# Attention, routed experts and a Fourier block on one core: softmax and weight decoding kept in PSUM, logits left in their scale, small work on ScalarE

## The chip, the cores and the metric

The kernel runs on one core of one Trainium2 chip. The metric is the device time of one execution in microseconds; what is compared is the median over runs. TensorE (PE) multiplies, VectorE (DVE), ScalarE (ACT) and GpSimd (POOL) work on tiles of up to 128 partitions, and SyncE (SP) issues most of the DMAs. Matrix results land in PSUM, in eight banks of 512 f32 columns; everything else lies in SBUF.

## The reference

Three blocks follow one another, on 8 batches of 576 rows with 8 heads of 64 columns (512 in all):

```python
# 1: attention against keys and values that are means over 8 rows (72 of them)
k_p, v_p = mean of 8 rows of k, v
scores = q @ k_p.T / 8;  attn = softmax(scores) (the sum has 1e-9 added);  x = attn @ v_p
# 2: one expert per row
logits = x @ w_gate                        # 8 experts
fresh = argmax(logits);  e = fresh where row 0 or sigmoid(x @ w_local) < 0.5, else that of the row before
p = softmax(logits);     out = p[e] * (relu(x @ w1[e]) @ w2[e])
# 3: Fourier mixing and a feed-forward block
u = out + real(fft over rows and columns of out);  un = layernorm(u)
result = u + relu(un @ w_ch1) @ w_ch2
```

The weights of block 3 arrive as 64-bit floats.

## The kernel before, in words

The program has two parts. **The first** does blocks 1 and 2 for batches 0 to 6, with the expert that the first row of a batch chooses; the attention of a batch runs beside the experts of the batch before. A loop over a number of further pairs of batch and expert, which is known only at run time, stands behind it. **The second** does the experts of batch 7, then block 3 batch by batch.

In the first part `moe` is a generator of 34 steps per batch, and `attention` one of some 21; the main loop advances the one beside the other, so the program's text interleaves them. The order on each engine is then set by a scheduler from the text and the data that each instruction needs. Each engine works through its order and waits in it.

Attention goes by five row tiles of 128 (one of 64). `att_A` turns q by TensorE and copies it (L225). `att_B` multiplies with the pooled keys into the tile `sc`, two PSUM banks with one buffer (L234 to L236), and forms the softmax on VectorE: maximum (L239), difference into the SBUF tile E (L242), Exp on ScalarE in place (L244), sum (L246), the addition of 1e-9 and a scale (L247), reciprocal (L248) and product (L249). For batches from 1 on, the result is split into a high half in f16 (ScalarE, L255) and a low half (VectorE, L256), and a DMA turns both (L258). `att_D` multiplies with V, `att_L` forms eight logits and the local gate's (L303, L304) and scales them by the column iv (L305). `route` chooses the experts from them, compares the gate with a constant (L336) and forms the softmax over experts (L341). L372 to L376 give each row its coefficient.

Experts: `moe1_f` multiplies with w1 in high and low halves into a bank of the tag `mm` (two buffers); ScalarE writes the high half of the result (L460), VectorE the low one (L461), which frees the bank. `moe2_t` multiplies with w2, `store_y` scales by the coefficient (L514), copies columns 0 and 256 into `ycol` (L515), and stores. The coefficients are scaled three times per batch first (L556). Meanwhile expert weights of the next batch are loaded, their maximum taken (VectorE, L401), scaled and rounded (ScalarE, L427, L428), and their low halves formed on POOL (L429). `pool_kv` forms the pooled keys and values on POOL (L169 to L171).

Decoding: five times per batch, `decode_parts` turns a piece of 64-bit weights into f32 by integer operations: Abs on ScalarE (L629), a maximum that also keeps the largest (L631), shift and mask (L632), and two merges with the upper and lower words (L634, L635), all in the SBUF tile dt; the next piece is loaded behind that (L616).

In PSUM the first part holds `mm` twice, `a1` twice, `sc` (two banks), `hg`, and `et`, which only batch 0 uses.

Of the kernel before, what the change touches and what calls it, by code (L numbers as in the profile page):

```python
# [9 lines left out]
F32 = mybir.dt.float32  # L10
# [13 lines left out]
E_TOP = 14  # L24
# [39 lines left out]
def attention_moe_fourier_kernel(ctx: ExitStack, tc: tile.TileContext, aps, out, B=8):  # L64
# [43 lines left out]
    def small(shape, dt, tag):  # L108
        return sm.tile(shape, dt, tag=tag, name=tag)
# [8 lines left out]
    wg_inv = const.tile([128, 1], F32, name="wg_inv")  # L118
    eps = const.tile([128, 1], F32, name="eps")
# [30 lines left out]
    kraw, kp, kbd, vs, vmax = {}, {}, {}, {}, {}  # L150
# [38 lines left out]
    def prep_v(b):  # L189
# [11 lines left out]
        TS(out=inv, in0=inv, scalar1=0.125, scalar2=None, op0=ALU.mult)  # L201

# [28 lines left out]
    def att_B(b, i):  # L231
# [8 lines left out]
        e = mt([128, 8, 72], F32, "E")  # L240
        e4 = e[:n].rearrange("p (a h) k -> p a h k", a=2)
        TT(out=e4, in0=s4, in1=mx[:n].to_broadcast([n, 2, 4, 72]), op=ALU.subtract)  # L242

        S.activation(out=e[:n], in_=e[:n], func=ACTF.Exp, scale=2.0 ** -6)  # L244
        es = small([128, 8, 1], F32, "es")
        V.tensor_reduce(out=es[:n, :, 0], in_=e[:n], axis=AX.X, op=ALU.add)  # L246
        TS(out=es[:n], in0=es[:n], scalar1=1e-9, scalar2=2.0 ** -E_TOP if b else 1.0, op0=ALU.add, op1=ALU.mult)  # L247
        V.reciprocal(out=es[:n], in_=es[:n])  # L248
        V.tensor_tensor(out=e[:n], in0=e[:n], in1=es[:n].to_broadcast([n, 8, 72]), op=ALU.mult)  # L249
        if b == 0:  # L250
            E[b, i] = e
            return
        hl = ehl_t[n_e[0] % 2]
        n_e[0] += 1
        S.copy(out=hl[:n, 0, :, 0:72], in_=e[:n])  # L255
        V.tensor_tensor(out=hl[:n, 1, :, 0:72], in0=e[:n], in1=hl[:n, 0, :, 0:72], op=ALU.subtract)  # L256
# [38 lines left out]
    def att_L(b, i):  # L295
# [9 lines left out]
        TS(out=lg[b][:n, i, :], in0=lg[b][:n, i, :], scalar1=iv[b][:n], scalar2=None, op0=ALU.mult)  # L305
# [19 lines left out]
    def route(b):  # L325
# [10 lines left out]
        TS(out=m, in0=lg[b][:, :, 8], scalar1=GATE_THR, scalar2=None, op0=ALU.is_le)  # L336
# [4 lines left out]
        S.activation(out=ex, in_=ex, func=ACTF.Exp)  # L341
# [4 lines left out]
        er = sm.tile([1, 576], F16, tag="r_er", name="r_er", bufs=1)  # L346
        n0 = 0
        for r, n in ((row, 320), (row2, 256)):
            mb = sm.tile([1, 320], F32, tag="r_mb", name="r_mb", bufs=1)
# [155 lines left out]
    def store_y(b, add):  # L505
        def done(i, n, po, c):
# [8 lines left out]
            V.tensor_copy(out=ycol[:n, i, :, b], in_=t[:n, 0:512:256])  # L515
# [4 lines left out]
    def moe(b, decs=()):  # L520
# [34 lines left out]
        for s in (p_all[:, b, 5:6], wsc[b, 0][0], wsc[b, 1][0]):  # L555
            TS(out=c, in0=c, scalar1=s, scalar2=None, op0=ALU.mult)  # L556
# [710 lines left out]
```

## Time and profile before

| | us |
|---|---|
| median of 3 runs (1571.8 to 1578.5) | 1575.95 |
| the profiled execution | 1575.51 |
| its span, first to last instruction | 1573.6 |
| VectorE busy | 1141.8 (73%) |
| TensorE busy, matmul | 1369.7 (87%) |
| ScalarE busy | 562.0 (36%) |
| POOL busy | 407.5 (26%) |

The span is that of the profiled execution; 1.9 us lie around it. An engine's busy time is a sum over stages with different limits, so a stage is read by itself, with its own windows and waits. In the timelines and groups, a line such as "E<-sc,mx" names the tile written and those read. An instruction's duration holds the time in which it stood still after its start.

### The profile page before, as it was taken

The numbers are of one execution on the slowest core, as the hardware profiler recorded it, in microseconds if no ns is written. First come the engines' busy times: TensorE is split into PE (matmuls) and PEld (weight loads), VectorE is DVE, ScalarE is ACT, GpSimd is POOL, SyncE is SP. The second block draws the span as 40 slices with busy tenths as digits, with TensorE's granted clock in tenths as the row PEclk, the third lists the DMA queues.
The fourth block names the chain that finished last, engine by engine and source line by source line (L and its number), as shares of the span: only waits on it lengthen the run. The fifth ranks groups of instructions, "written<-read, shape, count | busy, mean of one in ns | idle before, by whom it ended". The sixth has DMA issues, their size and how long they took to land.

```text
span 1573.6 us, 25049 instructions
## 1 busy us (share of the span) xinstructions
PE 1369.7 (87%) x9674; PEld 846.5 (54%) x9674; DVE 1141.8 (73%) x2292; ACT 562.0 (36%) x1007; POOL 407.5 (26%) x465
## 2 busy tenths in 40 slices
PE   3777888778878889679499999999999999999997
PEld 3444444344434545245356666666666666666664
DVE  5896999988989988648487667575668666577442
ACT  1354555444636465525242222222222122223120
POOL 3562726363675322245301001010101001000000
PEclk9688989888988999888799999999999999999999
DMA  8648568677886757343835335160704325153010
GB/s 162 191 121 231 147 207 212 186 190 208 197 228 165 204 155 233 97 139 108 134 99 108 54 70 92 51 110 21 123 20 104 59 67 95 50 133 76 11 44 27
DMA packets 245954, 193.97 MB, mean 123 GB/s; under 512 B 185255, under 2 KB 191271, under 8 KB 244807
## 3 DMA queue, kind: packets, MB, share of 16 engines
q1 hardware_dynamic: 230198, 172.21, 45.0%
q0 software_dynamic: 10272, 10.41, 2.7%
q10 hardware_dynamic: 5360, 9.70, 1.7%
q8 instruction: 78, 1.28, 0.3%
q14 instruction: 46, 0.37, 0.1%
HBM read 111.83 MB, written 47.37 MB: 101 GB/s over the span
## 4 chain that ended last, share of the span: by engine, by line
PE 47%; DMA 6%; DVE 2%; issue 1%; ACT 0%; SPq 0%; DVEq 0%; ACTq 0%
PE mm L914 19%; PE s L981 10%; PE et L981 5%; PE hg L981 5%; DMA xhl<-un 3%; PE a L864 2%; PE mm L456 2%; DMA out_dram<-c 2%; PE a L863 1%; PE a L871 1%; DMA dd<-fw_dram 1%; PE a L752 1%; DVE c L919 0%; PE hg L457 0%; DMA c<-u_dram 0%
## 5 line engine op out<-in xcount | busy, mean ns | idle before, releaser
L919 DVE TENSOR_TENSOR c<-mm,c 128x512 f32<-128x512 f32 x180 | 122.6, 686 | 151.1 <-PE mm L914 146.1
L456 PE MATMUL mm<-xhl,w0h 128*128 128x512 f16 x512 | 178.7, 417 | 57.9 <-DVE hl L461 33.3
L914 PEld LDWEIGHTS <-wr 128*128 128x128 f16 x1728 | 168.9, 98 | 61.9 <-issue 24.0
L766 POOL DMA_DIRECT2D yb<-y_dram x42 | 26.8, 651 | 477.3 <-DVE pt L816 391.9
L914 PEld LDWEIGHTS <-ex 128*128 128x128 f16 x1296 | 125.6, 98 | 24.6 <-issue 5.7
L981 PEld LDWEIGHTS <-hl 128*128 128x128 f16 x864 | 83.8, 98 | 94.9 <-issue 1.6
L981 PEld LDWEIGHTS <-hh 128*128 128x128 f16 x864 | 84.5, 98 | 88.5 <-issue 2.4
L914 PE MATMUL mm<-xhl,wr 128*128 128x256 f16 x864 | 107.5, 275 | 23.8 <-DMA xhl<-un 23.8
L924 ACT COPY c<-mm 128x512 f32<-128x512 f32 x72 | 41.4, 584 | 183.7 <-PE mm L914 158.9
L914 PE MATMUL mm<-xhl,ex 128*128 128x256 f16 x864 | 106.6, 274 | 0.0
L456 PE MATMUL mm<-xhl,w0l 128*128 128x512 f16 x256 | 106.1, 414 | 0.1
L456 PEld LDWEIGHTS <-w0h 128*128 128x128 f16 x512 | 53.0, 104 | 96.2 <-issue 47.9
L930 ACT ACTIVATE hl<-c 128x512 f16<-128x512 f32 x72 | 45.3, 629 | 163.8 <-DVE c L919 163.8
L486 PE MATMUL mm<-w1h,hh 128*128 128x512 f16 x256 | 99.0, 387 | 1.0 <-DVE hl L461 0.9
L486 PE MATMUL mm<-w1h,hl 128*128 128x512 f16 x256 | 98.6, 385 | 0.0
L486 PE MATMUL mm<-w1l,hh 128*128 128x512 f16 x256 | 98.6, 385 | 0.0
L429 POOL TENSOR_TENSOR w0l<-wr,w0h 128x512 f16<-128x512 f32 x56 | 67.2, 1223 | 115.3 <-ACT w0h L428 29.6
L457 PE MATMUL hg<-xhl,w0h 128*128 128x64 f16 x512 | 91.9, 205 | 0.0
L930 ACT ACTIVATE hh<-c 128x512 f16<-128x512 f32 x72 | 44.6, 629 | 119.3 <-DVE c L919 119.2
L427 ACT ACTIVATE wr<-wr,wscale 128x512 f32<-128x512 f32 x120 | 79.9, 712 | 14.7 <-DVE wscale L134 11.9
L429 POOL TENSOR_TENSOR w1l<-wr,w1h 128x512 f16<-128x512 f32 x64 | 73.0, 1168 | 33.9 <-ACT w1h L428 26.5
L401 DVE TENSOR_REDUCE wmax<-wr 128x1 f32<-128x1024 f32 x64 | 76.8, 1208 | 2.0 <-DMA wr<-in_moe_w_dram 2.0
(294 smaller groups left out, 3229.9 us busy)
## 6 DMA issues: line engine op xcount, KB each, us to landing
wr<-in_moe_w_dram SPq DMA_DIRECT2D x32, 1024.0 KB
dd<-in_moe_w_ch_dram SPq DMA_DIRECT2D x32, 512.0 KB
kraw<-in_k_dram SPq DMA_DIRECT2D x8, 1152.0 KB
vraw<-in_v_dram SPq DMA_DIRECT2D x8, 1152.0 KB
xs_dram<-xhl SPq DMA_DIRECT2D x8, 1152.0 KB
y_dram<-y ACTq DMA_DIRECT2D x32, 256.0 KB
fw_dram<-dt SPq DMA_DIRECT2D x32, 256.0 KB
u_dram<-yb SPq DMA_DIRECT2D x32, 256.0 KB
```

Of the source, the lines that this page charges most:

```text
L401: V.tensor_reduce(out=m[:, c:c + 1], in_=tc_, axis=AX.X, op=ALU.max, apply_absolute_value=True)
L427: S.activation(out=t[:, sl], in_=t[:, sl], func=ACTF.Copy, scale=s)
L429: G.tensor_tensor(out=l[:, sl], in0=t[:, sl], in1=h[:, sl], op=ALU.subtract)
L456: P.matmul(po, lhsT=ww[:, c], rhs=x[:, j, kk, 64:576], start=st, stop=sp)
L457: P.matmul(go, lhsT=ww[:, c], rhs=x[:, j, kk, 0:64], start=st, stop=sp)
L486: P.matmul(po, lhsT=hx[:, f, c0:c0 + n], rhs=ww[:, 512 * f:512 * f + 512], start=(f == 0 and t == 0), stop=(f == 7 and t == 2))
L864: P.matmul(o, lhsT=fd[2][gw, n, :M], rhs=tabs[nm][gw, 1, i], start=False, stop=True)
L914: P.matmul(o[:, q], lhsT=fw1[n][:, w, kk, f], rhs=unT[b][x][:, u, kk, :], start=(kk == 0 and i == 0), stop=(kk == 1 and i == 2))
L919: TT(out=c, in0=x, in1=y, op=ALU.add)
L924: S.copy(out=c, in_=o)
L930: S.activation(out=d[0], in_=c, func=ACTF.Relu)
L981: P.matmul(acc[i], lhsT=h[:, x, hf, q, 128 * i:128 * i + 128], rhs=fw2[w][hf][:, 512 * f:512 * f + 512], start=(f == 0 and hf == 0 and n = ...
```

## The change

Five edits, all in the first part's functions:

- `att_B` keeps difference, Exp, sums and product in the PSUM tile `sc`; only batch 0 writes its result into SBUF. The split reads PSUM, and `sc` comes free with the low half.
- `decode_parts` works in a PSUM bank of the tag `et` (one buffer); only the last merge writes SBUF.
- The logits keep their scale: the instruction of L305 goes. The gate's threshold is scaled for each batch instead (one product of two columns, and one for all), and the routing's Exp takes iv as its scale.
- The columns for `ycol` and the three scalings of the coefficients go from VectorE to ScalarE.
- Three small tiles of the routing move from the lasting pool to that of the first part.

```diff
-        e = mt([128, 8, 72], F32, "E")
-        e4 = e[:n].rearrange("p (a h) k -> p a h k", a=2)
-        TT(out=e4, in0=s4, in1=mx[:n].to_broadcast([n, 2, 4, 72]), op=ALU.subtract)
-        S.activation(out=e[:n], in_=e[:n], func=ACTF.Exp, scale=2.0 ** -6)
-        es = small([128, 8, 1], F32, "es")
-        V.tensor_reduce(out=es[:n, :, 0], in_=e[:n], axis=AX.X, op=ALU.add)
-        TS(out=es[:n], in0=es[:n], scalar1=1e-9, scalar2=2.0 ** -E_TOP if b else 1.0, op0=ALU.add, op1=ALU.mult)
-        V.reciprocal(out=es[:n], in_=es[:n])
-        V.tensor_tensor(out=e[:n], in0=e[:n], in1=es[:n].to_broadcast([n, 8, 72]), op=ALU.mult)
+        TT(out=s4, in0=s4, in1=mx[:n].to_broadcast([n, 2, 4, 72]), op=ALU.subtract)
+        S.activation(out=sc[:n, :, 0:288], in_=sc[:n, :, 0:288], func=ACTF.Exp, scale=2.0 ** -6)
+        sums = sc[:n, 0, 288:296]
+        V.tensor_reduce(out=sums.rearrange("p (a h) -> p a h", a=2), in_=s4, axis=AX.X, op=ALU.add)
+        TS(out=sums, in0=sums, scalar1=1e-9, scalar2=2.0 ** -E_TOP if b else 1.0, op0=ALU.add, op1=ALU.mult)
+        es = small([128, 2, 4, 1], F32, "es")
+        V.reciprocal(out=es[:n].rearrange("p a h o -> p (a h o)"), in_=sums)
         if b == 0:
-            E[b, i] = e
+            E[b, i] = e = mt([128, 8, 72], F32, "E")
+            TT(out=e[:n].rearrange("p (a h) k -> p a h k", a=2), in0=s4, in1=es[:n].to_broadcast([n, 2, 4, 72]), op=ALU.mult)
             return
+        TT(out=s4, in0=s4, in1=es[:n].to_broadcast([n, 2, 4, 72]), op=ALU.mult)
...
-        S.copy(out=hl[:n, 0, :, 0:72], in_=e[:n])
-        V.tensor_tensor(out=hl[:n, 1, :, 0:72], in0=e[:n], in1=hl[:n, 0, :, 0:72], op=ALU.subtract)
+        hi, lo = (hl[:n, x, :, 0:72].rearrange("p (a h) k -> p a h k", a=2) for x in range(2))
+        S.copy(out=hi, in_=s4)
+        TT(out=lo, in0=s4, in1=hi, op=ALU.subtract)
...
+        TT(out=thr[b], in0=s, in1=wg_thr, op=ALU.mult)
...
-        TS(out=lg[b][:n, i, :], in0=lg[b][:n, i, :], scalar1=iv[b][:n], scalar2=None, op0=ALU.mult)
...
-        TS(out=m, in0=lg[b][:, :, 8], scalar1=GATE_THR, scalar2=None, op0=ALU.is_le)
+        TS(out=m, in0=lg[b][:, :, 8], scalar1=thr[b], scalar2=None, op0=ALU.is_le)
...
-        S.activation(out=ex, in_=ex, func=ACTF.Exp)
+        S.activation(out=ex, in_=ex, func=ACTF.Exp, scale=iv[b])
...
-            V.tensor_copy(out=ycol[:n, i, :, b], in_=t[:n, 0:512:256])
+            S.copy(out=ycol[:n, i, :, b], in_=t[:n, 0:512:256])
...
-            TS(out=c, in0=c, scalar1=s, scalar2=None, op0=ALU.mult)
+            S.activation(out=c, in_=c, func=ACTF.Copy, scale=s)
...
-        S.activation(out=t.bitcast(F32), in_=hi.bitcast(F32), func=ACTF.Abs)
+        pf = bank([128, 512], "et")
+        pi = pf.bitcast(I32)
+        S.activation(out=pf, in_=hi.bitcast(F32), func=ACTF.Abs)
...
-        TS(out=t.bitcast(F32), in0=t.bitcast(F32), scalar1=TINY_HI, scalar2=0.0, op0=ALU.max, op1=ALU.max, accum_out=fmax[:, c:c + 1])
-        TS(out=t, in0=t, scalar1=3, scalar2=0x3FFFFFF8, op0=ALU.logical_shift_left, op1=ALU.bitwise_and)
+        TS(out=pf, in0=pf, scalar1=TINY_HI, scalar2=0.0, op0=ALU.max, op1=ALU.max, accum_out=fmax[:, c:c + 1])
+        TS(out=pi, in0=pi, scalar1=3, scalar2=0x3FFFFFF8, op0=ALU.logical_shift_left, op1=ALU.bitwise_and)
...
-        STT(out=t, in0=hi, scalar=-0x40000000, in1=t, op0=ALU.bitwise_and, op1=ALU.bitwise_or)
-        STT(out=t, in0=lo, scalar=29, in1=t, op0=ALU.logical_shift_right, op1=ALU.bitwise_or)
+        STT(out=pi, in0=hi, scalar=-0x40000000, in1=pi, op0=ALU.bitwise_and, op1=ALU.bitwise_or)
+        STT(out=t, in0=lo, scalar=29, in1=pi, op0=ALU.logical_shift_right, op1=ALU.bitwise_or)
```

The scheduler gives each engine of the first part another order. VectorE before, in batch 4, between the products of the second and third row tile's softmax (the L249 is the second tile's, L239 and L242 the third's; E and ehl hold the softmax and its halves):

```order
L249 TENSOR_TENSOR E<-E,es 128x576
L365 COPY code_all<-a_3507 64x1
L515 COPY ycol<-y 128x2
L635 SCALAR_TENSOR_TENSOR dt<-dd,dt 128x512
L371 TENSOR_TENSOR r_oh<-tab_81,code_all 128x40
L239 TENSOR_REDUCE mx<-sc 128x8
L256 TENSOR_TENSOR ehl_97<-E,ehl_97 128x8x72
L372 TENSOR_TENSOR r_oh<-r_oh,r_ex 128x40
L242 TENSOR_TENSOR E<-sc,mx 128x576
```

VectorE with the change, at the same place (L248 to L261 the second tile's, L242 the third's; lines are those of the changed kernel, where L248 is the sum, L256 the product, L261 the low half, and L637 to L640 decode):

```order
L248 TENSOR_REDUCE sc<-sc 128x8
L249 TENSOR_SCALAR sc<-sc 128x8
L251 RECIPROCAL es<-sc 128x8
L256 TENSOR_TENSOR sc<-sc,es 128x2x288
L637 TENSOR_SCALAR et,fmax<-et 128x512
L261 TENSOR_TENSOR ehl_98<-sc,ehl_98 128x8x72
L638 TENSOR_SCALAR et<-et 128x512
L640 SCALAR_TENSOR_TENSOR et<-dd,et 128x512
L242 TENSOR_REDUCE mx<-sc 128x8
L641 SCALAR_TENSOR_TENSOR dt<-dd,et 128x512
L244 TENSOR_TENSOR sc<-sc,mx 128x2x288
```

Before, the third tile's maximum stands ahead of the second's low half; now it stands behind it, since the scores of a tile enter `sc` only when the low half before has been read. The copy of `ycol` is gone from between. On TensorE some 30 large multiplications of the experts (tag `mm`) now stand between the scores of two tiles of one batch, on average over the 28 such pairs of batches 1 to 7, where it was 24.

ScalarE before, in batch 4, from the second tile's Exp (L244) to the scaling of expert weights (L427):

```order
L629 ACTIVATE dt<-dd 128x512
L244 ACTIVATE E<-E 128x576
L514 ACTIVATE y<-mm,cm 128x512
L225 COPY qT<-a_3495 128x512
L517 DMA y_dram<-y 128x512
L427 ACTIVATE wr_3016<-wr_3016,wscale_3489 128x512
L255 CAST ehl_97<-E 128x8x72
```

ScalarE with the change, about the same place (L635 is decoding's Abs, L246 the Exp, L260 the high half, L519 the `ycol` copy, L560 the scaling of the coefficients):

```order
L518 ACTIVATE y<-mm,cm 128x512
L519 COPY ycol<-y 128x2
L521 DMA y_dram<-y 128x512
L246 ACTIVATE sc<-sc 128x2x288
L560 ACTIVATE cm<-cm,p_all 128x5
L560 ACTIVATE cm<-cm,winv_3179 128x5
L635 ACTIVATE et<-dd 128x512
L260 CAST ehl_98<-sc 128x8x72
```

The copies now follow the scaling L518 ahead of its store, and the scalings of the coefficients stand ahead of an Abs and a high half in ScalarE's queue.

## Rows read from the trace of the kernel before

**Rows 1.** Stretches: busy us (instructions) of PE, PEld, DVE, ACT, POOL; granted clock; DMA share; GB/s.
```profile
90.00:655.00 565.00, 463.60 (x3712) 253.69 (x3708) 501.53 (x1043) 298.25 (x528) 261.39 (x266) 0.90 0.70 190
...
800.00:1573.00 773.00, 755.45 (x4974) 497.61 (x4971) 491.05 (x950) 184.78 (x324) 39.07 (x68) 1.00 0.33 70
```

**Rows 2.** Waits of TensorE, 90 to 655 us: us in total, times, longest.
```profile
PE mm L456 <- DVE hl L461: 33.3, 9, 10.2
PE a L285 <- DVE vs L413: 12.0, 5, 3.1
PE a L285 <- ACT vs L412: 11.3, 3, 6.6
PE a L303 <- DVE xhl L290: 10.2, 8, 3.0
PE sc L236 <- DVE E L242: 6.1, 4, 2.8
```

**Rows 3.** Groups of VectorE, 90 to 655 us: busy us, mean ns, idle time before.
```profile
L634 DVE SCALAR_TENSOR_TENSOR dt<-dd,dt 128x512 int32<-128x512 int32 x32 | 31.7, 991 | 0.1
L256 DVE TENSOR_TENSOR ehl<-E,ehl 128x576 f16<-128x576 f32 x28 | 27.7, 990 | 2.7 <-ACT ehl L255 2.4
L635 DVE SCALAR_TENSOR_TENSOR dt<-dd,dt 128x512 int32<-128x512 int32 x32 | 24.8, 774 | 0.1
L249 DVE TENSOR_TENSOR E<-E,es 128x576 f32<-128x576 f32 x28 | 23.7, 847 | 0.1
L631 DVE TENSOR_SCALAR_CACHE_REDUCE dt<-dt 128x512 f32<-128x512 f32 x32 | 21.8, 680 | 21.4 <-ACT dt L629 21.2
L556 DVE TENSOR_SCALAR cm<-cm,winv 128x5 f32<-128x5 f32 x16 | 21.3, 1330 | 0.3
L242 DVE TENSOR_TENSOR E<-sc,mx 128x576 f32<-128x576 f32 x28 | 21.0, 749 | 0.3
...
L305 DVE TENSOR_SCALAR lg<-lg,iv 128x9 f32<-128x9 f32 x28 | 19.1, 682 | 0.1
...
L632 DVE TENSOR_SCALAR dt<-dt 128x512 int32<-128x512 int32 x32 | 16.8, 524 | 0.2
L247 DVE TENSOR_SCALAR es<-es 128x8 f32<-128x8 f32 x28 | 11.6, 414 | 0.1
L515 DVE COPY ycol<-y 128x2 f32<-128x2 f32 x28 | 9.2, 327 | 4.1 <-ACT y L514 4.1
L556 DVE TENSOR_SCALAR cm<-cm,p_all 128x5 f32<-128x5 f32 x8 | 7.3, 915 | 0.0
L305 DVE TENSOR_SCALAR lg<-lg,iv 64x9 f32<-64x9 f32 x7 | 7.0, 996 | 0.0
...
L299 DVE TENSOR_TENSOR iv<-p_all,wg_inv 128x1 f32<-128x1 f32 x7 | 4.0, 565 | 0.0
```

**Rows 4.** Timeline of VectorE, 192 to 204 us: start, length.
```profile
192.56 9.40 DVE L556 TENSOR_SCALAR cm<-cm,winv 128x5 f32<-128x5 f32 x2
```

**Rows 5.** Timeline of POOL, the same stretch.
```profile
196.34 6.70 POOL L429 TENSOR_TENSOR w1l<-wr,w1h 128x512 f16<-128x512 f32 x6
```

**Rows 6.** One line, whole span: minimum, median and maximum ns.
```profile
L247 DVE TENSOR_SCALAR es<-es x40: 133/164/1239, 31.9 to 609.5; 128x8 f32<-128x8 f32 x32, 64x8 f32<-64x8 f32 x8
```

**Rows 7.** Group of ScalarE, 90 to 655 us: busy us, mean ns, idle time before.
```profile
L341 ACT ACTIVATE r_ex<-r_ex 128x40 f32<-128x40 f32 x7 | 1.7, 237 | 2.4 <-DVE r_ex L340 2.3
```

**Rows 8.** Timeline of VectorE, low half of two tiles.
```profile
89.21 0.74 DVE L256 TENSOR_TENSOR ehl<-E,ehl 64x576 f16<-64x576 f32 x1
...
591.04 0.75 DVE L256 TENSOR_TENSOR ehl<-E,ehl 128x576 f16<-128x576 f32 x1
```

**Rows 9.** Timeline of TensorE, scores of three tiles.
```profile
83.06 1.23 PE L236 MATMUL sc<-kbd,qT 128*128 128x144 f32 x8
...
577.32 1.22 PE L236 MATMUL sc<-kbd,qT 128*128 128x144 f32 x8 [1.54 <-DVE code_all L365]
...
590.23 1.25 PE L236 MATMUL sc<-kbd,qT 128*128 128x144 f32 x8
```

More of the change, by code (lines that the diff above doesn't have):

```diff
@@ L118, in attention_moe_fourier_kernel @@
     wg_inv = const.tile([128, 1], F32, name="wg_inv")
+    wg_thr = const.tile([128, 1], F32, name="wg_thr")
     eps = const.tile([128, 1], F32, name="eps")
@@ L147, in absmax @@
         return across(m, tag)
-    kraw, kp, kbd, vs, vmax = {}, {}, {}, {}, {}
+    kraw, kp, kbd, vs, vmax, thr = {}, {}, {}, {}, {}, {}
     def load_kv(b):
@@ L201, in prep_v @@
         TS(out=inv, in0=inv, scalar1=0.125, scalar2=None, op0=ALU.mult)
+        thr[b] = small([128, 1], F32, "thr")
+        TT(out=thr[b], in0=s, in1=wg_thr, op=ALU.mult)
     qt, qT, E, ET, xhl, lg, iv = {}, {}, {}, {}, {}, {}, {}
@@ L345, in route @@
             P.matmul(r[:, s0:s0 + n], lhsT=f16[:n, j:j + 1], rhs=ident16[:n, :n], start=True, stop=True)
-        er = sm.tile([1, 576], F16, tag="r_er", name="r_er", bufs=1)
+        er = pool["sb"].tile([1, 576], F16, tag="r_er", name="r_er", bufs=1)
         n0 = 0
         for r, n in ((row, 320), (row2, 256)):
-            mb = sm.tile([1, 320], F32, tag="r_mb", name="r_mb", bufs=1)
+            mb = pool["sb"].tile([1, 320], F32, tag="r_mb", name="r_mb", bufs=1)
             TS(out=mb[:, 0:n], in0=r[:, 0:n], scalar1=0.0, scalar2=None, op0=ALU.is_equal)
@@ L1035, in count_extras @@
     def count_extras():
-        oh = sm.tile([128, B, 5, 8], F32, tag="x_oh", name="x_oh", bufs=1)
+        oh = pool["sb"].tile([128, B, 5, 8], F32, tag="x_oh", name="x_oh", bufs=1)
         cnt = small([128, B, 8], F32, "x_cnt")
@@ L1071, in attention_moe_fourier_kernel @@
     pow2_scale(absmax(wg_raw, 128), wg_inv, s, 0)
+    TS(out=wg_thr, in0=s, scalar1=8.0 * GATE_THR, scalar2=None, op0=ALU.mult)
     split(wg_hl[:, :, 0], wg_hl[:, :, 1], wg_raw, s)
```

## The prediction, as it was put on record

> **What bounds the kernel now.** I read the stretches first. The first part, from 90 us to 655 us, has VectorE busy for 501.5 of 565 us and TensorE for 463.6 at a granted clock of 0.90; from 800 us on TensorE is busy for 755.5 of 773 us at full clock [rows 1]. The change touches the first part alone, so the end part stays as it is, and the question is what 565 us become.
>
> Second, who waits for whom. Of TensorE's 101.4 us of idle time in that stretch (565 less 463.6), 33.3 us ended with VectorE's low half of the hidden rows (L461), 12.0 with the low half of V (L413), 10.2 with the low half of x (L290) and 6.1 with the subtraction that frees the score banks (L242): 61.6 us. A further 11.3 us ended with the scaling of V on ScalarE, which takes its scale from VectorE [rows 2]. So VectorE is the engine that the others wait for, but it is not the only bound: TensorE has 82% of the stretch itself.
>
> Third, what VectorE spends its time on. The two kinds of small scaling, on 9 and 5 columns, take 682 to 1330 ns each, as long as a subtraction of 576 columns does (749) [rows 3]. The timeline shows why: from 192.56 us two scalings of five columns took 9.40 us together, to 201.96, while POOL ran six subtractions of weights back to back from 196.34 to 203.04 (1.12 us each), behind additions; the second scaling got through as the fifth of the six ended [rows 4, 5]. L249 and L256 with both inputs in SBUF average 847 and 990 ns, though L242, with one input in PSUM, takes 749 for the same width [rows 3]. So VectorE stands still beside POOL in instructions that read two SBUF tensors and in the small ones that scale one, and those that read PSUM are spared: no group of rows 3 with a PSUM input has such a mean. [...]
>
> **The sum on VectorE, in this stretch** [rows 3, 6]:
> - L305, scaling of the logits, is gone: 19.1 + 7.0 = 26.1 us.
> - L556, 24 scalings of the coefficients, goes to ScalarE: 21.3 + 7.3 = 28.6 us.
> - L515, kept columns, goes to ScalarE: 9.2 us for the full tiles. Together 63.9 us.
> - L247 on PSUM: 28 x 414 ns become 28 x 164, its median, for its work is the same and only POOL's share goes: 7.0 us.
> - L249 and L256: to 749 ns, L242's price: 23.7 + 27.7 become 2 x 21.0, so 9.4 us. L242 and the reductions have one SBUF input already: nothing.
> - L634 and L635: 31.7 + 24.8 become 2 x 32 x 680 ns = 43.5, so 13.0 us (680 is L631's price at this width).
> - L632 gets dearer. In SBUF it has 524 ns on average; nothing in this trace runs it in PSUM, and the nearest row, on the same tile and of the same width, is L631 with 680: 32 x 156 ns = 5.0 us more. The bounds are 0 more and 32 x 467 = 14.9 more (L634's 991).
> - Added: the gate's threshold, one product of two SBUF columns per batch, like L299: 7 x 565 ns = 4.0 us. The one for all batches is a single small instruction ahead of the stretch.
>
> That is 63.9 + 7.0 + 9.4 + 13.0 - 5.0 - 4.0 = 84.3 us of 501.5. For results that VectorE writes into PSUM the trace has no row; I take L242's price (PSUM in) and L631's (width), as the nearest. If PSUM were no better than today's means, the 29.4 us of the softmax and decoding terms would go and 54.9 would be left; below that nothing is known that would take more, save L632's bound.
>
> [...] L242 reads PSUM and takes 749 ns; L256, with both inputs in SBUF and the same width, took 740 and 750 ns where POOL left it alone [rows 3, 8], so a move into PSUM costs nothing that these rows show. [...]
>
> ScalarE takes the 24 scalings and 34 copies at about 237 ns, the price of its small Exp (L341): 13.7 us beside 298 us of work in 565 [rows 1, 7]. That hides in its idle 267 us; without that cover it would cost the 13.7. Its Exp, Abs and high half now read or write PSUM: I take no change, and bound it at a tenth of a us on 100 instructions, 10 us either way, under the same cover. The first scaling waits for the routing on VectorE, with casts, Abs and copies queued behind it on ScalarE; today the routing's Exp waits so, for 2.4 us in seven batches [rows 7]; even ten times that would fit into the idle time, and nothing is taken for it. The copies stand ahead of the stores of y, which no engine reads in this part. Decoding's single "et" bank costs nothing: the next piece of weights is loaded only behind L635, which ends the bank's use too. No DMA is added; SP's order moves transposes by a place or two.
>
> **What is late next.** The score banks were freed by L242; now they are held until the low half is written (L256's place). Today the next scores on TensorE start before that: by 6.9 us at the first pair of tiles of one batch, by 1.6 at the last of the 26 (of 28 pairs) where it is so [rows 8, 9]; over the 28 pairs it is 155 us, 5.5 each. That wait is new on TensorE, and matrix multiplications of the experts queue behind it. Three things take it back. The chain from the end of the scores to the low half's end, 13.3 us at the tile of 577.32 us [rows 8, 9] and 14 on average over 35, loses its own 0.6 us (16.4 us over 28 tiles); as VectorE's queue has 17% less work in it, the rest falls by about 2.2 us; and the new order of instructions puts on average 30 instead of 24 large multiplications between two such scores, 1.5 us or so. What is left is 1.0 to 1.2 us per pair, and I take 1.0: 28 us.
>
> So on the path: TensorE's 61.6 + 11.3 = 72.9 us of waits go, as VectorE gets 12 us of room in each of seven batches, and 28 us come: 45 us. 565 would become 520, with TensorE at 89% and VectorE at 80%, which is possible. The profiled execution took 1575.5 us (span 1573.6 and 1.9 around it), 0.4 under the median of the three runs: 1575.5 - 45 = 1530.5, say **1531 us**.
>
> **Rivals.**
> - *All of it passes.* If VectorE alone paces the stretch and TensorE's new wait hides in idle time, 84 us go: 1491; a rising granted clock (0.90 here) may add a few. For it: 89% busy. Against it: TensorE would have to be busy 96% of what is left.
> - *The waits move.* POOL's work stays, and other instructions with two SBUF inputs (the routing's, L331 to L376) meet the same rows of subtractions. The scalings' blocked part is about 45 us (54.7 less 59 instructions at 0.164, L247's median); if half comes back, the saving is 62 us, and TensorE's waits fall by 73 x 62/84 = 54; less the 28 of the new wait: 26 us, 1550. For it: what holds VectorE is POOL's work, which stays. Against it: few such instructions are left.
> - *The score banks become the bound: slower.* If the chain of the softmax stays as long as it is, for it waits on three queues, and only the order's 1.5 to 2 us help, each pair costs 3.5 us: 98 us of new waits against 73 gone, 25 us slower: 1600. It decides at 73/28 = 2.6 us per pair. For it: the score banks have one buffer. Against it: the order leaves six more multiplications between, and VectorE has less to do.
> - *No change.* If transfers pace it (their share is 0.70 over the stretch [rows 1]), idle time moves to them: 1570 to 1580. Against it: TensorE hardly waits for one.
>
> **Numbers.** A measurement of this kernel can tell about 0.5% (8 us) from no change. The forecast with 1510 to 1545: 0.45. All passes, 1486 to 1510: 0.16. Waits move, 1545 to 1567: 0.20. No change: 0.07. Slower: 0.12. So faster 0.81, same 0.07, slower 0.12. The range reaches from 1486, the full saving with a little clock, to 1572, which leaves out the slower case and little more.
>
> **What would show it.** Right: VectorE's busy time down by 70 to 95 us over the first part; L249, L256 and L634 at 680 to 760 ns without their outliers; L632 near 680; TensorE's wait for L461 under 15 us; scores waiting for the low half about 1 us a pair. The first part would end near 610 us, and the end part would not change. Wrong: the scores' wait above 2.6 us a pair, or small instructions of the routing that swell to several us beside POOL, or VectorE's softmax instructions in PSUM at over 850 ns.

## The result, and the profile after

| | before | changed |
|---|---|---|
| median | 1575.7 us | 1559.8 us (16 runs each) |
| ratio | | 0.991, 95% interval 0.9885 to 0.9936 |
| the profiled execution's span | 1573.6 us | 1553.5 us |
| VectorE busy, whole span | 1141.8 us | 1044.4 us |

The change makes the kernel about 16 us faster, where 45 us were forecast (1531 us). The time lies inside the range, and the saving is about a third of what was expected. The profiled execution of the changed kernel took 1555.3 us, 4.5 below the median (four of its 16 runs took 1571 to 1574), so the spans differ by 20.1 us where the medians differ by 15.9. The work of VectorE fell as forecast and a little more: 97.4 us less, where the sum gave 84.3. So the question is what became of it.

Three stretches behind the start tell it: the middle, from the first hidden rows that ScalarE writes to the end of the last scaling of y of batch 6; the change-over, from there to the first multiplication of batch 7; and the end part. The windows of these three, of the kernel before (columns: stretch, its length, then busy us and instructions of PE, PEld, DVE, ACT, POOL, granted clock, DMA share, GB/s):

```profile
79.30:656.20 576.90, 472.05 (x3809) 259.31 (x3806) 512.64 (x1062) 302.69 (x537) 268.92 (x276) 0.90 0.70 189
656.20:668.10 11.90, 0.03 (x1) 0.03 (x2) 1.18 (x12) 2.80 (x6) 1.86 (x3) 0.50 0.05 15
668.10:1573.60 905.50, 854.20 (x5592) 557.37 (x5592) 572.80 (x1106) 233.49 (x425) 98.97 (x141) 0.97 0.36 78
```

The same three of the changed kernel:

```profile
85.70:629.30 543.60, 458.31 (x3808) 251.49 (x3804) 411.96 (x960) 308.07 (x590) 235.38 (x265) 0.94 0.78 198
629.30:647.60 18.30, 0.02 (x1) 0.02 (x2) 4.09 (x19) 4.36 (x10) 4.29 (x6) 0.50 0.12 44
647.60:1553.50 905.90, 859.17 (x5592) 559.75 (x5592) 572.48 (x1102) 233.76 (x429) 99.54 (x141) 0.97 0.35 78
```

The middle stretch is 33.3 us shorter, with the same multiplications (3809 and 3808 in the records). 13.7 us of that is TensorE's busy time (472.05 to 458.31), at a granted clock of 0.94 instead of 0.90; 19.6 us is its idle time (104.9 to 85.3). Two stretches give back: the start is 6.4 us longer (79.3 to 85.7) and the change-over to batch 7 another 6.4 (11.9 to 18.3). The end part is unchanged. -33.3 + 6.4 + 6.4 + 0.4 = -20.1, the difference of the two spans.

VectorE's instructions have the durations of the forecast. Groups of VectorE in the changed kernel, 90 to 640 us (busy us, mean ns, idle time before); L637 to L641 decode, and the others are the softmax and its low half:

```profile
L637 DVE TENSOR_SCALAR_CACHE_REDUCE et<-et 128x512 f32<-128x512 f32 x32 | 22.2, 693 | 20.9 <-ACT et L635 20.7
L638 DVE TENSOR_SCALAR et<-et 128x512 int32<-128x512 int32 x32 | 22.1, 691 | 0.1
L640 DVE SCALAR_TENSOR_TENSOR et<-dd,et 128x512 int32<-128x512 int32 x32 | 22.0, 687 | 0.1
L641 DVE SCALAR_TENSOR_TENSOR dt<-dd,et 128x512 int32<-128x512 int32 x32 | 21.8, 681 | 0.0
...
L256 DVE TENSOR_TENSOR sc<-sc,es 128x576 f32<-128x576 f32 x28 | 21.3, 760 | 0.2
L261 DVE TENSOR_TENSOR ehl<-sc,ehl 128x576 f16<-128x576 f32 x28 | 21.1, 754 | 11.2 <-ACT ehl L260 11.0
L242 DVE TENSOR_REDUCE mx<-sc 128x8 f32<-128x576 f32 x28 | 21.1, 754 | 20.5 <-PE sc L239 20.1
...
L249 DVE TENSOR_SCALAR sc<-sc 128x8 f32<-128x8 f32 x28 | 4.7, 169 | 0.1
```

The merges were 991 and 774 ns and are 687 and 681; product and low half were 847 and 990 and are 760 and 754; the small addition was 414 and is 169 [rows 3]. The last column has VectorE waiting for ScalarE and TensorE now: it is no longer the engine that all others wait for.

These means hide that much of what TensorE gains lies in a few instructions. In the kernel before, L634 has a median of 682 ns, and one of its 32 stood for 10.26 us, from the middle of a run of POOL's additions and subtractions to just behind its end (at 284.33 us). TensorE's wait for the low half of the hidden rows ended behind it (first VectorE, then TensorE, of the kernel before):

```profile
274.62 10.26 DVE L634 SCALAR_TENSOR_TENSOR dt<-dd,dt 128x512 int32<-128x512 int32 x1
...
285.61 0.58 PE L456 MATMUL mm<-xhl,w0h 128*128 128x512 f16 x1 [10.16 <-DVE hl L461]
```

Three more such stand-stills, of one L556 (8.1 us) and two L305 (4.1 and 7.9), end in waits of 8.8, 4.8 and 6.4 us. So 30.1 of the 33.3 us that TensorE waited for L461 [rows 2] lie behind four instructions. The changed kernel has no VectorE instruction over 3.3 us in this part.

TensorE's waits in the changed kernel, 90 to 640 us (total, times, longest):

```profile
PE a L290 <- DMA ET<-ehl: 45.9, 16, 8.4
PE mm L460 <- DVE y L506: 7.8, 2, 6.0
PE sc L239 <- DVE ehl L261: 6.3, 6, 2.5
PE a L290 <- ACT vs L416: 4.9, 3, 2.0
PE mm L460 <- DVE hl L465: 4.0, 2, 2.4
...
PE a L308 <- DVE xhl L295: 1.9, 1, 1.9
```

L290 is the product with V, L465 the low half of the hidden rows. The five waits that the forecast counted as going, 72.9 us [rows 2], are down to 10.8 (4.9 + 4.0 + 1.9). But TensorE now stands in front of the product with V for 45.9 us, until the transposed halves have landed. In the kernel before, that wait had

```profile
PE a L285 <- DMA ET<-ehl: 2.4, 2, 1.9
```

The transposes themselves, 90 to 640 us, first of the kernel before, then of the changed one (min/median/max ns of one, as SyncE's queue issues it):

```profile
L258 SPq DMA_TRANSPOSE ET<-ehl x35: 1247/1950/6352, 90.0 to 613.7; - x35
```

```profile
L263 SPq DMA_TRANSPOSE ET<-ehl x35: 1247/3358/8681, 92.2 to 593.9; - x35
```

Taken tile by tile from the trace, the time from the end of a low half to the start of its product with V was 12.5 us on average over 35 tiles and is 10.3; issuing the transpose takes 2.7 and now 3.7 of it; and the time left behind that fell from 9.7 to 6.1 us (median 8.7 to 4.1). The shortest is about 2 us in both kernels; in the changed one, the 16 products that waited for the landing itself started 1.9 to 4.4 us behind the end of the issue.

The longer change-over shows in the timeline of VectorE of the changed kernel (start, length, and the idle time before):

```profile
615.15 0.70 DVE L637 TENSOR_SCALAR_CACHE_REDUCE et<-et 128x512 f32<-128x512 f32 x1 [1.82 <-ACT et L635]
...
623.06 0.70 DVE L637 TENSOR_SCALAR_CACHE_REDUCE et<-et 128x512 f32<-128x512 f32 x1 [3.00 <-ACT et L635]
...
631.02 0.70 DVE L637 TENSOR_SCALAR_CACHE_REDUCE et<-et 128x512 f32<-128x512 f32 x1 [2.72 <-ACT et L635]
...
638.16 0.15 DVE L131 TENSOR_SCALAR amr<-amr 128x1 f32<-128x1 f32 x1 [3.94 <-POOL amr L139]
```

The last pieces of weights are decoded 8 us apart, as their loads arrive (ScalarE's L635 waited 1.0, 0.3 and 1.1 us for them, until 614.5, 622.4 and 630.4), and the maximum over all of them follows at 638. The experts of batch 6 are done at 629.3, but batch 7 begins only when this is done too. In the kernel before, the last piece was decoded at 653.8, ahead of the last y at 656.2.

### The profile page after: what moved, and what is told of

It reads as the page before. It is cut to its first block, busy times and chain, and to the rows that moved or that the text cites. A ratio compares the mean times of both kernels' runs of the same rounds, so it can differ in the third digit from the quotient of the medians.

```text
span 1553.5 us, 24994 instructions
## 1 busy us (share of the span) xinstructions
PE 1360.3 (88%) x9674; PEld 842.6 (54%) x9674; DVE 1044.4 (67%) x2197; ACT 569.3 (37%) x1071; POOL 383.5 (25%) x465
## 4 chain that ended last, share of the span: by engine, by line
PE 47%; DMA 5%; DVE 3%; issue 1%; SPq 1%; ACT 1%; POOL 0%; DVEq 0%; ACTq 0%
PE mm L920 18%; PE s L987 11%; PE et L987 6%; PE hg L987 5%; DMA out_dram<-c 2%; PE mm L460 2%; PE a L870 2%; PE a L869 1%; PE a L877 1%; DMA xhl<-un 1%; DMA dd<-fw_dram 1%; PE a L758 1%; SPq L993 0%; SPq L817 0%; DMA ab<-un 0%
## 5 line engine op out<-in xcount | busy, mean ns | idle before, releaser
L460 PE MATMUL mm<-xhl,w0h 128*128 128x512 f16 x512 | 172.9, 406 | 32.9 <-POOLq L1112 21.0
L920 PEld LDWEIGHTS <-wr 128*128 128x128 f16 x1728 | 168.9, 98 | 60.1 <-issue 22.1
L987 PEld LDWEIGHTS <-hh 128*128 128x128 f16 x864 | 84.6, 98 | 86.7 <-issue 0.5
L461 PE MATMUL hg<-xhl,w0h 128*128 128x64 f16 x512 | 84.5, 197 | 0.0
L433 POOL TENSOR_TENSOR w0l<-wr,w0h 128x512 f16<-128x512 f32 x56 | 63.3, 1155 | 69.4 <-ACT wr L431 23.0
L490 PEld LDWEIGHTS <-hh 128*128 128x128 f16 x512 | 48.9, 99 | 53.4 <-issue 4.2
```

The lines of the kernel that those rows point to most:

```text
L433: G.tensor_tensor(out=l[:, sl], in0=t[:, sl], in1=h[:, sl], op=ALU.subtract)
L460: P.matmul(po, lhsT=ww[:, c], rhs=x[:, j, kk, 64:576], start=st, stop=sp)
L461: P.matmul(go, lhsT=ww[:, c], rhs=x[:, j, kk, 0:64], start=st, stop=sp)
L490: P.matmul(po, lhsT=hx[:, f, c0:c0 + n], rhs=ww[:, 512 * f:512 * f + 512], start=(f == 0 and t == 0), stop=(f == 7 and t == 2))
L920: P.matmul(o[:, q], lhsT=fw1[n][:, w, kk, f], rhs=unT[b][x][:, u, kk, :], start=(kk == 0 and i == 0), stop=(kk == 1 and i == 2))
L987: P.matmul(acc[i], lhsT=h[:, x, hf, q, 128 * i:128 * i + 128], rhs=fw2[w][hf][:, 512 * f:512 * f + 512], start=(f == 0 and hf == 0 and n = ...
```

## The experiments

Four parts of the change are taken apart: the softmax in place (with low half), decoding in place, the logits left in their scale with the moves to ScalarE ("small work"), and the routing tiles' pool, which goes with all. Intervals are of the ratio to the kernel before, at 95%.

### The parts

**Softmax back in SBUF** (the rest of the change stays):

```diff
-        TT(out=s4, in0=s4, in1=mx..., op=ALU.subtract)
-        S.activation(out=sc[:n, :, 0:288], in_=sc[:n, :, 0:288], func=ACTF.Exp, ...)
+        TT(out=e4, in0=s4, in1=mx..., op=ALU.subtract)
+        S.activation(out=e[:n], in_=e[:n], func=ACTF.Exp, ...)
...
```

> The change without its softmax part: difference and product go to SBUF again, so the score banks come free with the difference. Theory A (holding the score banks until the low half is written strings the tiles' softmax chains one behind the other, and TensorE then waits for the transposed halves): TensorE's wait for ET, 46 us in the changed kernel, falls under 15 us, and the time is 1530 to 1550, though VectorE gets some 15 us of standing still back. Theory B (VectorE was not the pace; transfers are): the wait for ET stays above 30 us and the time within 8 us of the change, 1552 to 1568.

1550.5 us, ratio 0.9837 (0.981 to 0.9864): faster than the whole change. Its waits of TensorE, 90 to 640 us:

```profile
PE a L306 <- DVE xhl L293: 19.8, 8, 8.9
PE mm L458 <- DVE hl L463: 17.6, 9, 5.1
...
PE a L288 <- DMA ET<-ehl: 1.8, 2, 1.2
```

Most of the waits for VectorE are back, as its softmax stands still beside POOL again (VectorE busy 1101.1), and the wait for the transposed halves is gone. The first hidden rows come at 77.9 us instead of 85.7. In this order of instructions, then, the softmax in place costs 9 us net. Whether it does so in another is tried below.

**Softmax in place alone** (the kernel before with that part):

> The kernel before with the softmax part alone. Theory A: the chains are strung up and VectorE is hardly relieved (15 us), so no gain or a loss: 1575 to 1600, with TensorE's waits on ET and the low half above 40 us together. Theory B: 15 us of VectorE's time pass in part, 1562 to 1576.

1588.2 us, 1.0068 (1.0049 to 1.0088): slower than before. TensorE's longest wait, and two groups of VectorE, 90 to 655 us (L306 scales the logits, L633 is decoding's shift and mask):

```profile
PE sc L236 <- DVE ehl L257: 60.3, 13, 14.6
```

```profile
L633 DVE TENSOR_SCALAR dt<-dt 128x512 int32<-128x512 int32 x30 | 43.8, 1459 | 0.2
L306 DVE TENSOR_SCALAR lg<-lg,iv 128x9 f32<-128x9 f32 x28 | 33.3, 1191 | 0.1
```

Two things are to be seen. VectorE saves nothing (busy 1140.0): the means of L306 and L633 are 1191 and 1459 ns, where they were 682 and 524 [rows 3]. Their medians are 228 and 426 ns; what fills the means is two stand-stills of each, of 10.8 to 15.8 us. The longest lasted while POOL ran 16 instructions without a pause. So the standing still beside POOL went from the softmax to instructions that were left in SBUF, and got longer. And the wait for the score banks is mostly this: three of the 13 waits, 42.7 of the 60.3 us, lie behind a stand-still of L633, L633 and L306. One of them, on VectorE and then on TensorE:

```profile
292.44 13.82 DVE L633 TENSOR_SCALAR dt<-dt 128x512 int32<-128x512 int32 x1
...
308.11 1.33 PE L236 MATMUL sc<-kbd,qT 128*128 128x144 f32 x4 [14.56 <-DVE ehl L257]
```

The other 17.6 us are 0.6 us per pair of tiles. So the held banks let a VectorE that stands still reach TensorE's scores, and cost little there by themselves. What the total lost is in the start: the first hidden rows come at 93.8 us instead of 79.3, and the middle is 3 us longer than before.

**The change without decoding in place:**

> The change with decoding left in SBUF. Both theories: VectorE loses 8 us of its saving and has 30 us and more of idle time to take it in, 1558 to 1570. If decoding's single bank held something up, it is faster than the change: under 1552.

1575.0 us, 1.0004 (0.9979 to 1.003): nothing is left of the gain, where 1558 to 1570 was expected. Two groups of VectorE, 90 to 655 us:

```profile
L635 DVE TENSOR_SCALAR dt<-dt 128x512 int32<-128x512 int32 x31 | 45.1, 1455 | 0.2
L321 DVE SCALAR_TENSOR_TENSOR fe_c<-lg,fe_m,tab 1x8 f32<-1x8 f32 x7 | 26.4, 3768 | 0.2
```

Shift and mask in SBUF takes the standing still once more (20.9 and 10.0 us in two instructions), and so does L321, an instruction on eight elements in the choice of the batch's expert, with 3768 ns (10.5 and 9.7 us in two of seven). In the whole change, as L322, it has 1043.

**Small work alone** (logits, moves to ScalarE, no part in place):

```diff
-        TS(out=lg[b][:n, i, :], in0=lg[b][:n, i, :], scalar1=iv[b][:n], ..., op0=ALU.mult)
...
-            V.tensor_copy(out=ycol[:n, i, :, b], in_=t[:n, 0:512:256])
+            S.copy(out=ycol[:n, i, :, b], in_=t[:n, 0:512:256])
...
```

> Only logits left in their scale, coefficients and kept columns on ScalarE; softmax and decoding as before. 64 us of VectorE's time go, by the prediction's rows. Theory A: most of the change's gain and more, 1530 to 1555. Theory B: 1555 to 1570.

1568.7 us, 0.9943 (0.9922 to 0.9965). VectorE is busy for 37 us less, where the removed instructions had 63.9. Groups, 90 to 655 us (L259 the low half, L252 the product):

```profile
L259 DVE TENSOR_TENSOR ehl<-E,ehl 128x576 f16<-128x576 f32 x28 | 37.3, 1333 | 5.9 <-ACT ehl L258 5.5 <-ACT hh L462 0.3
L252 DVE TENSOR_TENSOR E<-E,es 128x576 f32<-128x576 f32 x28 | 28.4, 1014 | 0.1
```

They had 990 and 847 [rows 3]. As a sum over VectorE up to 665 us, what each instruction takes beyond the shortest of its kind (where that is over 150 ns) is 121.5 us before, 115.9 with the softmax alone, 91.7 without decoding, 95.5 with the small work alone, 86.8 without the softmax, and 24.0 with the whole change. So the parts don't add up: while instructions that stand still beside POOL are left, much of the saving turns up in them.

### The places where time was given back

**Product to SBUF.** The last product of the softmax writes E in SBUF, so the score banks come free before the halves are formed:

```diff
-        TT(out=s4, in0=s4, in1=es[:n]..., op=ALU.mult)
+        e = mt([128, 8, 72], F32, "E")
+        TT(out=e4, in0=s4, in1=es[:n]..., op=ALU.mult)
...
```

> The change, but the softmax product goes from PSUM to SBUF, so the score banks come free one product earlier, before the two halves. Theory A (the strung chain through the one buffer of scores sets the wait for the transposed halves): each of 28 chains is about 2.5 us shorter, TensorE's wait for ET falls from 46 us to under 30, and the time is 1545 to 1555. Theory B (the transposes' own way to landing sets it): the wait stays at 40 to 50 us, and the time at 1556 to 1566, with VectorE standing still some 7 us more in the low halves.

1556.5 us, 0.9893 (0.985 to 0.9937), which is not told apart from the change. The wait for the transposed halves falls by half, to 21.6 us, as theory A had it, and the one for the low half of the hidden rows is 24.0 instead of 4.0. Of that, 14.0 us lie behind one low half of the softmax, which reads SBUF alone again and stood for 15.1 us beside POOL.

**Transposes issued by ScalarE** instead of SyncE:

```diff
-        D.dma_start_transpose(out=ET[b, i]...
+        S.dma_start_transpose(out=ET[b, i]...
```

> The change with the transposing DMAs issued by ScalarE instead of SP. Theory B (SP's queue and its slow issue, 3.4 us in the median against 1.9 before, make the halves late): the wait for ET falls under 25 us and the time to 1540 to 1555, unless ScalarE pays for the issue. Theory A: the transposes start at once behind the low half already, so nothing is gained, and ScalarE is held by issues of several us: 1560 to 1590.

1608.8 us, 1.0225 (1.0187 to 1.0263). The wait is still 32.7 us. ScalarE's queue is held by each issue, for 1.3 to 10.4 us, and TensorE's waits for its x and scaled V are 13.6 and 12.8 us where they were 0.2 and 4.9. Taking the issue off SyncE costs more here than it brings.

**Batch 0 as before** (its softmax in SBUF, with `E` formed at once):

```diff
+        if b == 0:
+            E[b, i] = e = mt([128, 8, 72], F32, "E")
+            TT(out=e4, in0=s4, in1=mx..., op=ALU.subtract)
...
```

> The change with batch 0's softmax in SBUF as before. In the changed kernel the first hidden rows come 6.4 us later than before (85.7 against 79.3 us), since batch 0's five tiles have nothing else beside them. If the held score banks cause that, the first hidden rows come at 78 to 81 us and the time falls by 5 to 8 us: 1551 to 1556. If not, 1558 to 1562.

1570.0 us, 0.9978 (0.9951 to 1.0004). The start is won back: first hidden rows at 77.5 us. The total is 10 us worse, where at worst 1562 was expected, since batches behind it are longer; scores now wait 15.4 us for the low half where it was 6.3 (8.5 of it behind one stand-still of 9.4 us on the eight elements, L332 here), and the product with V 15.0 for the scaled V where it was 4.9.

**Decode loads one piece further ahead** (with a second buffer):

```diff
-        load_f64(c + 1)
+        load_f64(c + 2)
...
```

> The change with two buffers for the 64-bit pieces, loaded one piece ahead (batch 0's softmax result lies in other idle tiles to make room). In the changed kernel TensorE stands still for 21 us between the parts, with the last decodings each 8 us apart behind their loads. If those loads set the end of the first part, the pause falls to 13 us or less, ScalarE's wait for dd (31 us) goes, and the time is 1545 to 1555. If the pause comes from elsewhere, 1556 to 1564.

1566.9 us, 0.9962 (0.9938 to 0.9986), above the 1545 to 1564 that was expected. TensorE's wait at the change-over, of this kernel and, for the changed one, behind it (L1112 is the loop between the parts):

```profile
PE mm L459 <- POOLq L1112: 10.1, 1, 10.1
```

```profile
PE mm L460 <- POOLq L1112: 21.0, 1, 21.0
```

That fits loads that pace the change-over, but does not show it: batch 6 ended later here (the last y ends at 654.8 us instead of 629.2), so decoding had more time, too. There were 22.4 us of waits at the scores, where it was 6.3, and 14.9 of them lie behind a single VectorE instruction, again the one on eight elements (VectorE, then TensorE):

```profile
173.24 15.54 DVE L321 SCALAR_TENSOR_TENSOR fe_c<-lg,fe_m,tab 1x8 f32<-1x8 f32 x1
...
189.50 2.29 PE L239 MATMUL sc<-kbd,qT 128*128 128x144 f32 x8 [14.86 <-DVE ehl L260]
```

**Product with V a step later**, with a fourth buffer for the transposed halves (batch 0's E takes buffers of the hidden rows to make room):

```diff
-... "ET": 3, ...
+... "ET": 4, ...
-LAGS = ((1, 2, 3, 4), (1, 9, 4, 5))
+LAGS = ((1, 2, 3, 4), (1, 9, 5, 6))
```

> The change with the product with V of each tile put one round later in the text (and its logits with it), with four buffers for the transposed halves; batch 0's softmax result lies in other idle tiles to make room. Followed back from the end of the first part, the chain of waits of the changed kernel goes through landings of transposed halves for 102 us. Theory A+B (the strung softmax and the transposes' 6 us to landing make TensorE stand still in front of that product): the wait for ET, 46 us, falls under 15 us and the time is 1530 to 1550. Theory C (any order of this first part has about as much standing still, only elsewhere): the wait goes, others come, and the time is 1552 to 1575.

1556.8 us, 0.9877 (0.9855 to 0.9899). The wait for the halves falls to 24.2 us, those at the scores rise to 21.5 (14.7 behind a stand-still of 15.4 us of the same L321), and those for the scaled V are 13.5 and 5.5. On TensorE the product hardly moved: 55.7 large multiplications (tag `mm`) stand on average between a tile's scores and its product with V, and 54.6 in the next kernel. The buffers alone, as its control:

> Beside the run before: its four buffers and the moved softmax result of batch 0, with the product with V where the change has it. Theories A and B: the same as the change, 1553 to 1567, with TensorE's wait for ET at 35 us or more. Theory C: anything within 15 us of the change, as the order is set anew.

1559.2 us, 0.99 (0.9864 to 0.9936), with 43.4 us of that wait: the change over again.

Three of these did what they were made for at their own place (the product in SBUF, batch 0, and, as far as can be told, the loads), and each found another wait, a good part of it one VectorE instruction that met a run of POOL's work. That made the order itself suspect: each edit has the scheduler set a new order on all engines, and the order decides who meets whom.

### Orders of the same instructions

`AHEAD` (42) is the number of attention's steps by which the program's text runs ahead of the experts; where an expectation calls it the scheduler's look-ahead, this is meant. Another value changes no instruction, only how the text interleaves the two, and so the order that the scheduler sets:

```diff
-WAIT_W, AHEAD = 6, 42
+WAIT_W, AHEAD = 6, 44
```

> The kernel before with attention two steps further ahead of the experts (44 instead of 42), no other edit: how far a neutral shift of the order moves the time. If the order as such matters little, within 5 us of before; theory C: by 5 to 20 us, either way.

> The changed kernel with the same shift, 44 instead of 42. If order matters little, within 5 us of the change; theory C: 5 to 20 us off, either way, and not by the same amount as before's.

The kernel before has 1572.1 us under 44 (0.9976, 0.9961 to 0.9992), the change 1572.6 (0.9987, 0.9967 to 1.0006): 13 us above itself under 42, and no gain. The next three repeat the pair with and without the softmax part:

> The changed kernel with its softmax in SBUF as before, and the scheduler's look-ahead 44 in place of 42 (another order of the same instructions). It pairs with the whole change under 44 (1572.6 us). Theory (the softmax in place costs about 10 us because it holds the score banks through the softmax and so delays scores, low half and transposes): it is again faster than the whole change under the same number by 5 to 20 us, about 1555 to 1567. Rival (the 10 us between the two at 42 are the luck of one order): the sign or the size has nothing to do with that at 42; a difference of 0 or the other way is as likely, 1572 to 1585.

> The changed kernel with its softmax in SBUF, look-ahead 40. Pairs with the next run. Theory: 5 to 20 us faster than the next run, TensorE hardly waits for transposed halves (under 8 us). Rival (luck of one order): as fast or slower than the next run.

> The whole change, look-ahead 40. By how much it differs from 1560 us shows how far an order of the same instructions moves the time (I expect 1550 to 1575). Theory: TensorE's wait for the transposed halves is above 30 us here too, and it is 5 to 20 us slower than the run with the softmax in SBUF under 40. Rival (luck of one order): no such difference.

With the softmax back in SBUF it is 1570.8 us under 44 and 1578.5 under 40; the whole change has 1572.6 and 1576.3. So the 9 us between the two under 42 do not repeat (1.8 under 44, the other way by 2.3 under 40): the expectation that the part costs 5 to 20 us falls. The last three complete four pairs:

> The kernel before under look-ahead 40 (another order of the same instructions). With the runs under 42 and 44 it gives what the change is worth for three orders each. Theory (the change takes 97 us off VectorE but what that is worth on the path is a few us to 16, by the order): 1570 to 1590, so that the whole change under 40 (1576.3) stands 0 to 15 us below it. Rival (the change as such is worth 16 us, and 40 is a poor number for both): 1588 to 1596. Second rival (the change as such is worth nothing): 1560 to 1570.

> The kernel before under look-ahead 38: a fourth order. 1565 to 1595 by every theory; it pairs with the next run.

> The whole change under look-ahead 38. Theory (worth a few us to 16, by the order; the wait for the transposed halves comes in every order): 0 to 16 us below the run before it, TensorE's wait for the transposed halves 30 us or more. Rival (worth 16 us as such): 12 to 20 us below it. Second rival (worth nothing): within 4 us on either side or above it.

The kernel before under 40 and 38 has 1614.8 and 1597.3 us; both lie above every range that was expected for them. All of them, before / changed. Median times; the rest in us, from each one's profiled execution: the start up to the first hidden rows, from there to the last y of batch 6, the change-over to batch 7, and the wait for the transposed halves between 90 and 640 us.

| `AHEAD` | median | difference | start | middle | change-over | halves |
|---|---|---|---|---|---|---|
| 42 | 1575.7 / 1559.8 | -15.9 | 79.3 / 85.7 | 576.9 / 543.6 | 11.9 / 18.3 | 2.4 / 45.9 |
| 44 | 1572.1 / 1572.6 | +0.5 | 79.5 / 86.4 | 578.1 / 557.8 | 10.3 / 23.6 | none / 47.5 |
| 40 | 1614.8 / 1576.3 | -38.5 | 79.5 / 85.2 | 607.2 / 559.0 | 22.1 / 29.1 | 1.8 / 30.5 |
| 38 | 1597.3 / 1602.0 | +4.7 | 79.6 / 86.1 | 590.2 / 576.7 | 23.1 / 21.4 | 5.8 / 50.1 |

The rows of that wait, changed kernel under 44, 40 and 38:

```profile
PE a L289 <- DMA ET<-ehl: 47.5, 15, 9.3
```

```profile
PE a L289 <- DMA ET<-ehl: 30.5, 12, 6.5
```

```profile
PE a L289 <- DMA ET<-ehl: 50.1, 14, 9.6
```

What repeats in all four orders: VectorE's busy time falls (by 97, 74, 74 and 69 us), the middle gets shorter (by 33, 20, 48 and 14, of which TensorE's idle time is 20, 18, 41 and 15), the start is 6 to 7 us longer, and the wait for the transposed halves comes. What doesn't repeat is the 13.7 us of TensorE's busy time (2.0, 6.8, and 1.2 the other way in the other three), the change-over, and the total: from -39 to +5 us, -12 on average, with a spread between orders (a standard deviation of 20) that is larger than that. From four orders, -12 is not told apart from nothing, and four neighbouring values of one setting are no random sample. The best of the four is 1572.1 us before and 1559.8 changed. The end part, which the change does not touch, adds to the scatter: it is within 4 us in three pairs, and 7.9 us longer in the changed kernel's profile under 38. The 16 us are what the change is worth in the order that is set for it as it stands.

## Why the prediction was right or wrong

**The sum on VectorE was right.** 84.3 us were forecast, 97.4 came. The moved instructions have the prices that were taken from the nearest rows: L249 169 ns (164 forecast), L256 and L261 760 and 754 (749), the merges 687 and 681 (680), L638 691 (680; it is the term that got dearer). ScalarE's 59 new instructions take 13.8 us in all, from their groups, where 13.7 were taken, and they hide. ScalarE's Exp, Abs and high half, bounded at a tenth of a us of change, have medians of 635, 632 and 636 ns where they had 683, 667 and 672. That writing into PSUM costs VectorE no more than reading from it was a choice between bounds, and it held to 14 ns: the difference, which read PSUM before and now writes it as well (L244), went from 749 to 763 ns.

**What the moves into PSUM cost by themselves.** The low half, a subtraction of 576 columns, took 740 to 750 ns in SBUF [rows 8], with nothing on POOL's timeline at either time; it and the product take 754 and 760 from PSUM: some 5 to 20 ns more. Shift and mask took 524 ns on average in SBUF [rows 3], with a median of 422, and takes 691 in PSUM. That it would get dearer at all, the sum's 5.0 us, was the author's estimate from the price of L631: no row of the kernel before shows it in PSUM. In the changed kernel its group is 5.3 us dearer (16.8 to 22.1); for what reason, no run shows.

**That VectorE stands still beside POOL** was read right from rows 4 and 5, with two things missed. The means were read as the price of each instruction, and they are few long stand-stills: L305, at 682 and 996 ns, has a median of 232 and a maximum of 7905. So the waits at L461 did not go because VectorE got 12 us of room in each batch; 30.1 of their 33.3 us went with four stand-stills. And who is held up is not a property of the instruction alone. Where only some were taken away, others stood longer, up to 20.9 us. That is the mechanism of the rival "The waits move". It held for the softmax alone, the change without decoding, and the small work alone. The whole change has few such instructions left and only one stand-still over 3 us; its time lies in that rival's bracket (1545 to 1567) for another reason, and in three of the later variants its one instruction on eight elements took 9 to 15 us back. With the softmax alone in place, one stand-still of 15.8 us ran on over 16 of POOL's instructions.

**The step that failed is "What is late next".** It said: "What is left is 1.0 to 1.2 us per pair, and I take 1.0: 28 us", at the scores, and from that "72.9 us of waits go ... and 28 us come: 45 us". The first half held: 62.1 of the 72.9 us went. At the scores only 6.3 us came for the low half, 0.2 per pair, for the chain from the end of the scores to the low half's end fell from 14.1 to 9.6 us on average over 35 tiles, where 2.8 were taken off. What was late next stood one step behind: the product with V, which waits for the transposed halves. 43.5 us came there that the sum did not hold, and TensorE's idle time in the middle fell by 19.6 us instead of 45. The forecast took nothing for it ("SP's order moves transposes by a place or two"): the wait of the kernel before was 2.4 us, but what was left behind the issue had a median of 8.7 us, and could be used up.

What used it up is in the order. The forecast counted as a gain that 30 instead of 24 large multiplications stand between two tiles' scores. The scores moved back by this, and the product with V did not move with them: on average 66.4 large multiplications stood between a tile's scores and its product with V, and 54.6 stand there now. In all twelve kernels with the softmax in place it is 51 to 57, and in all eight with it in SBUF 66 to 75. The wait goes with it: 10.5 us where the softmax is the only part and 21.6 to 50.1 in the other eleven, against none to 5.8 us in the eight. The longer issue of the transposes does not repeat: its mean under 44, 40 and 38 is 3.3, 3.2 and 3.6 us before and 3.5, 3.4 and 3.7 with the change. That less of this wait would be a gain in the total is not shown; no run moved the product back by itself.

**Two places were not in the sum at all.** The start: batch 0's tiles follow one another with nothing between, so that held score banks string them out, 6 to 7 us in every order; with batch 0 in SBUF the first hidden rows come at 77.5 us again. And the change-over: when the batches end sooner, the decode loads end last. Against that, 13.7 us came unasked as TensorE's busy time fell at a granted clock of 0.94 instead of 0.90, which the forecast had allowed "a few" for, in a rival. Much of that was luck: the other orders have 2.0, 6.8, and 1.2 the other way.

**The rivals.** "All of it passes" fell, as TensorE was not bound by VectorE alone. "The score banks become the bound" has the right sign for the softmax alone (slower by 0.7%), but not the mechanism: 42.7 of the 60.3 us at the scores lie behind three stand-stills, and the rest is 0.6 us per pair where 3.5 were priced. "No change" is the total of the change under 44 (0.03%) and 38 (0.3%). It named transfers as the cause, and TensorE's largest wait is now one for a DMA, though because the product stands closer and not because the transposes got slower. That the order alone could decide had no place among the rivals.

## What to carry to other kernels

When a busy engine gets free, price the next meeting point of each chain that it feeds, by the time that is left there in the trace and not by the wait that is there today: a transfer that nobody waits for has room that can be used up (here a median of 8.7 us, down to 4.1). Read the longest instructions of a group, not its mean: here four stand-stills made 30 us of TensorE's longest wait, and when some of the instructions that stood still were taken away, others met the other engine's runs of work, for up to 20.9 us. Where a scheduler sets the order anew, run the kernel before and the change under several orders: here the order of the same instructions moved the time by up to 43 us, and a gain of 16 us is smaller than that.

## What the runs showed of the hardware that was not expected

A transpose by DMA holds the queue that issues it for 1.2 to 8.7 us in these two kernels (medians 1.95 us before and 3.36 after; the kernel before under 44 has 3.19). And one VectorE instruction on eight elements of one partition stood for 15.5 us while POOL ran additions and subtractions without a pause, and for 10.5 us where decoding was left in SBUF; its shortest in the changed kernel took 215 ns.

The fastest kernel of the study is the one with its softmax back in SBUF, 1550.5 us against 1559.8 and 1575.7. Under 44 and 40 it has 1570.8 and 1578.5, so that its lead belongs to one order as well.
